# Block 0's loads of v placed ahead of the first pieces of w_in in the SyncE queue

## The chip, the cores and the metric

The kernel runs on one core of a Trainium2 chip. The metric is device time in microseconds (us) of one execution. A trace of one execution is taken with the hardware profiler; its span is about 1.75 us shorter than the time that is reported for the same execution. Such a profile of one execution is called a look below. PE is TensorE (matmul), PEld its weight loads, ACT ScalarE, DVE VectorE, POOL GpSimd, SP SyncE and SPq its queue of DMA issues.

## The reference

Attention inside chunks of 64 tokens, then a two-layer network with a gated activation on all 4608 tokens:

```python
# q, k, v: (8, 8, 576, 64); chunks of 64 tokens, no attention across chunks
scores = scale * np.matmul(q_c, k_c.transpose(0, 1, 2, 4, 3))
attn = np.exp(scores - np.max(scores, axis=-1, keepdims=True))
attn = attn / (np.sum(attn, axis=-1, keepdims=True) + 1e-09)
x = np.matmul(attn, v_c)         # reordered to (4608, 512)
...
h = x @ w_in                     # w_in: (512, 2048)
g = h * (1.0 / (1.0 + np.exp(-beta * h)))
out = g @ w_out                  # w_out: (2048, 512)
```

## The kernel before

The kernel is a list of events, each with a time on a fictive clock. Sorted by that time they give the program of every engine; waits on semaphores are derived from reads and writes. Tokens are worked in nine blocks of 512. Block 0 has to begin before its data are there, so its loads stand in the queue of SyncE in the order of need. v of block 0 is loaded in eight pieces of 128 KB: four for the heads of the first half (u=0), four for the second (u=1). w_in is loaded in column groups s of 512 columns; group 0 comes in four row pieces c of 256 KB, group 1 to 3 in two pieces of 512 KB each. The first piece of group 1 is called **e1a** below.

```python
for u in range(2):
    for m in range(4):
        at(-97.9, load_v_u, 0, m, u)            # eight pieces of v ...
    for c in ((0,), (1, 2, 3))[u]:
        at(-97.9, load_w_in, 0, c, 1)           # ... w_in piece 0 between the halves
for e0 in range(1, 4):
    for cp in range(2):
        at(-97.7, load_w_in, e0, 2 * cp, 2)     # groups 1 to 3; e1a is the first
...
for m in range(4):                              # POOL: casts to bf16
    at(8.6 + 0.1 * m - 100, cast_v_u, 0, m, 0, "pool")
    at(10.4 + 0.1 * m - 100, cast_v_u, 0, m, 1, "pool")
at(10 - 100, cast_w_in, 0, 0, ("pool",))
...
for t in range(4):                              # PE: first layer, group 0
    at(11.5 + 0.1 * t - 100, mm1, 0, t, (0,))   # after the attention of u=1 (11.21, 11.46)
    at(12.1 + 0.1 * t - 100, mm1, 0, t, (1,))
    at(14 + 0.5 * t - 100, mm1, 0, t, (2, 3))
```

PE works in program order: attention of u=1 (needs v, second half), then the four matmuls of w_in piece 0 and of piece 1 with the transposes of x between them, then pieces 2 and 3, then group 1.

The softmax here doesn't subtract the row's maximum and nothing guards it: scores larger than these inputs give would overflow.

## Time and profile before

| | before |
|---|---|
| time, median of 3 runs | 290.87 us (290.63 to 291.61) |
| profiled execution | 292.47 us, span 290.7 us |
| PE busy | 280.4 us, 96% of the span |
| last v piece of block 0 landed | 17.63 us |
| e1a landed | 22.04 us |

Busy time is time with an instruction on the engine; a busy PE can still be pipelined less than perfectly. The page also shows that the DMA engines carry more than the kernel's loads. It lists the DMA queues with their packets, bytes and share of the 16 engines' time:

```profile
q1 hardware_dynamic: 127264, 47.33, 74.5%
q10 hardware_dynamic: 5600, 9.84, 11.0%
q8 instruction: 17, 0.28, 0.5%
q14 instruction: 7, 0.06, 0.1%
```

q1 has SyncE's loads, q10 ACT's transfers, and the third line is 17 fetches of program code of 16 KB each. The first came at 15.06 us. The seven fetches of the last line have 8 KB each.

### The profile page before, as it was taken

How to read it: one execution, taken by the hardware profiler on the slowest of the kernel's cores; microseconds unless marked ns; L12 is line 12 of the kernel's file. 1: busy time of each engine (PE TensorE's matmuls, PEld its weight loads, DVE VectorE, ACT ScalarE, POOL GpSimd, SP SyncE). 2: the span in 40 equal slices, each digit the busy share in tenths (PEclk: the TensorE clock that was granted, in tenths of full speed). 3: DMA queues.
4: the chain of work that ended last, by engine and by line, in shares of the span. 5: the costliest groups of instructions: out<-in, count | busy, mean ns of one | idle time of the engine just before them, and what ended most of it. 6: DMA issues, size and time to landing. Idle time of an engine off the chain costs nothing.

```text
span 290.7 us, 5459 instructions
## 1 busy us (share of the span) xinstructions
PE 280.4 (96%) x2210; PEld 136.2 (47%) x2210; DVE 146.3 (50%) x289; ACT 159.0 (55%) x225; POOL 80.9 (28%) x126
## 2 busy tenths in 40 slices
PE   7669999999999999999999999999999999999995
PEld 3434445545544554445444544454445444544444
DVE  0736616585428452745285617561856086608601
ACT  2436606688247824782488347743874377528510
POOL 1548845734121442050114102410233020000000
PEclk9999999999999999999999999999999999999999
DMA  6999999999599999995999599949999891340033
GB/s 229 242 290 399 407 359 247 298 164 267 144 235 201 271 219 224 210 235 125 193 242 238 92 221 204 276 116 180 235 184 182 189 204 23 74 127 18 2 69 77
DMA packets 132888, 57.51 MB, mean 198 GB/s; under 512 B 116864, under 2 KB 123264, under 8 KB 132864
## 3 DMA queue, kind: packets, MB, share of 16 engines
q1 hardware_dynamic: 127264, 47.33, 74.5%
q10 hardware_dynamic: 5600, 9.84, 11.0%
q8 instruction: 17, 0.28, 0.5%
q14 instruction: 7, 0.06, 0.1%
HBM read 36.71 MB, written 9.44 MB: 159 GB/s over the span
## 4 chain that ended last, share of the span: by engine, by line
PE 90%; SPq 4%; DMA 3%; POOL 0%; issue 0%; ACT 0%; DVE 0%
PE F L492 42%; PE F L472 38%; PE A L472 4%; DMA wstage<-in_moe_w_in_dram 3%; PE A L408 2%; PE A L382 2%; SPq L354 2%; SPq L323 1%; PE F L517 1%; SPq L246 1%; PE A L340 1%; POOL w_in_bf L260 0%; ACT kT L258 0%; PE A L421 0%; PE F L451 0%
## 5 line engine op out<-in xcount | busy, mean ns | idle before, releaser
L492 PE MATMUL F<-w_out_bf,g 128*128 128x512 bf16 x560 | 129.2, 379 | 0.0
L485 DVE SCALAR_TENSOR_TENSOR g<-tt,F 128x512 bf16<-128x512 bf16 x132 | 89.9, 687 | 75.9 <-ACT tt L482 75.7
L472 PE MATMUL F<-xT,w_in_bf 128*128 128x512 bf16 x528 | 116.9, 379 | 0.2
L482 ACT ACTIVATE tt<-F,beta_half 128x512 bf16<-128x512 f32 x132 | 89.7, 687 | 26.9 <-PE F L472 26.8
L472 PEld LDWEIGHTS F<-xT,w_in_bf 128*128 128x128 bf16 x528 | 51.1, 98 | 61.9 <-issue 0.6
L492 PEld LDWEIGHTS F<-w_out_bf,g 128*128 128x128 bf16 x560 | 51.8, 98 | 56.4
L500 ACT ACTIVATE ostage<-F 128x512 f32<-128x512 f32 x33 | 19.6, 597 | 67.1 <-PE F L492 67.0
L260 POOL CAST vaug<-vstage 128x512 bf16<-128x512 f32 (+1 forms) x44 | 23.5, 537 | 80.1 <-DMA vstage<-in_v_dram 77.2
L403 ACT ACTIVATE wstage<-A 64x1024 bf16<-64x1024 f32 x28 | 28.5, 1018 | 5.2 <-PE A L382 4.7
L260 POOL CAST qcast<-qstage 128x1024 bf16<-128x1024 f32 (+1 forms) x18 | 17.0, 945 | 44.6 <-DMA qstage<-in_q_dram 43.5
L433 DVE TENSOR_TENSOR x_sb<-A,rden 128x256 bf16<-128x256 f32 (+1 forms) x62 | 27.9, 450 | 2.1
L431 DVE RECIPROCAL rden<-A 128x4 f32<-128x4 f32 (+1 forms) x62 | 11.2, 180 | 29.8 <-PE A L408 26.1
L260 POOL CAST kcast<-kstage 128x512 bf16<-128x512 f32 (+1 forms) x29 | 18.1, 628 | 25.2 <-DMA kstage<-in_k_dram 24.9
L408 PEld LDWEIGHTS A<-vaug,wstage 128*128 128x128 bf16 x224 | 10.8, 98 | 6.7 <-ACT wstage L403 1.7
L408 PE MATMUL A<-vaug,wstage 128*128 128x65 bf16 x224 | 11.7, 193 | 0.0
L472 PE MATMUL A<-xT,w_in_bf 128*128 128x512 bf16 x48 | 11.0, 379 | 0.2 <-POOL w_in_bf L260 0.2
L260 POOL CAST w_in_bf<-wstage 128x512 bf16<-128x512 f32 x16 | 9.5, 613 | 3.4 <-DMA wstage<-in_moe_w_in_dram 3.2
L482 ACT ACTIVATE tt<-A,beta_half 128x512 bf16<-128x512 f32 x12 | 8.0, 690 | 2.1 <-PE A L472 2.1
L485 DVE SCALAR_TENSOR_TENSOR g<-tt,A 128x512 bf16<-128x512 bf16 x12 | 7.8, 684 | 2.0 <-ACT tt L482 2.0
L260 POOL CAST w_out_bf<-wstage 128x1024 bf16<-128x1024 f32 x8 | 8.3, 1040 | 1.8 <-DMA wstage<-in_moe_w_out_dram 1.7
L382 PEld LDWEIGHTS A<-qT,kT 64*64 64x64 bf16 x576 | 6.2, 107 | 4.2 <-issue 3.0
L382 PE MATMUL A<-qT,kT 64*64 64x64 bf16 x576 | 7.5, 196 | 0.3 <-ACT kT L258 0.3
(52 smaller groups left out, 73.0 us busy)
## 6 DMA issues: line engine op xcount, KB each, us to landing
out_dram<-ostage ACTq DMA_DIRECT2D x32, 256.0 KB, 3.6
kstage<-in_k_dram SPq DMA_DIRECT2D x30, 256.0 KB, 6.5
qstage<-in_q_dram SPq DMA_DIRECT2D x12, 512.0 KB, 5.4
vstage<-in_v_dram SPq DMA_DIRECT2D x24, 256.0 KB, 4.9
wstage<-in_moe_w_out_dram SPq DMA_DIRECT2D x8, 512.0 KB, 12.6
vstage<-in_v_dram SPq DMA_DIRECT2D x24, 128.0 KB, 4.6
wstage<-in_moe_w_in_dram SPq DMA_DIRECT2D x6, 512.0 KB, 9.2
qstage<-in_q_dram SPq DMA_DIRECT2D x8, 256.0 KB, 9.0
```

Source lines behind the costliest of these rows:

```text
L260: P.op(eng, lambda e: e.tensor_copy(dst, src), reads=r, writes=wr)
L354: P.dma("sp", lambda e: e.dma_start(stages["v"][:, blk, 512 * m + 256 * u:512 * m + 256 * u + 256].rearrange("p (h d) -> p h d", d=64), v[ ...
L382: return e.matmul(A[64 * c2:64 * c2 + 64, bank, col:col + 64], turned["k"][r, hp, t], qq)
L403: P.op("act", lambda e: e.activation(dst, src, AF.Exp, scale=0.125), reads=[K("A", 2 * u + i, v=("s", blk)) for i in range(2)], writes=[K( ...
L408: P.op("pe", lambda e, h=h: e.matmul(A[:, bank, 128 * (h % 4):128 * (h % 4) + 65], EB[:, 16 * u + 8 * (h % 2) + 4 * (h // 2 % 2) + m, :], ...
L431: P.op("dve", lambda e: e.reciprocal(rd, o[:, :, :, 64]), reads=r, writes=[K("rden", m, u, v=blk) for m in ms])
L433: P.op("dve", lambda e: e.tensor_tensor(x_sb[:, ms[0]:ms[0] + n, 256 * u:256 * u + 256].rearrange("p b (h d) -> p b h d", h=4), o[:, :, :, ...
L472: P.op("pe", lambda e, c=c: e.matmul(ps[:, bank, :], w_in_bf[:, c, 256 * e0 + i:256 * e0 + 256:2], xT[:, c, :], start=(c == 0), stop=(c == ...
L482: P.op("act", lambda e: e.activation(tt[:, T % NTT, :], ps[:, bank, :], AF.Tanh, scale=beta_half[:, e0, i:i + 1]), reads=[K(*pkey(ps, bank ...
L485: P.op("dve", lambda e: e.scalar_tensor_tensor(g2[:, t, :], tt[:, T % NTT, :], 1.0, ps[:, bank, :], ALU.add, ALU.mult), reads=[K(*pkey(ps, ...
L492: P.op("pe", lambda e, t=t: e.matmul(F[:, s, :], g2[:, t, 128 * s:128 * s + 128], w_out_bf[:, t, :], start=(t == 0), stop=(t == NT - 1)), ...
L500: f = (lambda e: e.activation(dst, src, AF.Copy, scale=0.5)) if eng == "act" else \
```

## The change

The intent is to let the second half of v, which has attention, normalising and transposing behind it, go ahead of w_in piece 0. The cast of piece 0 moves behind the casts of v in POOL's program, and pieces 2 and 3 become one DMA.

```diff
         for u in range(2):
             for m in range(4):
                 at(-97.9, load_v_u, 0, m, u)
-            for c in ((0,), (1, 2, 3))[u]:
-                at(-97.9, load_w_in, 0, c, 1)
+        for c, n in ((0, 1), (1, 1), (2, 2)):
+            at(-97.8, load_w_in, 0, c, n)
...
-        at(10 - 100, cast_w_in, 0, 0, ("pool",))
+        at(11 - 100, cast_w_in, 0, 0, ("pool",))
```

The programs of PE, DVE and ACT are the same instruction for instruction.

## The prediction

> **What bounds the kernel now.** I read the page first: 290.7 us of span, PE (TensorE matmul) busy 280.4 us of it. Adding up the chain of work that ended last gives PE for 90% and the queue of SyncE (SPq) with its transfers for 7%. That 7% lies at the front, so I then read the chain in order of time from the start of the span to 26 us (columns: start us, us, what):
>
> ```profile
> 6.54 2.10 SPq L354
> 8.68 1.53 SPq L246
> ...
> 12.39 0.93 SPq L246
> ...
> 14.34 7.70 DMA wstage<-in_moe_w_in_dram
> 22.04 0.05 issue
> 22.09 1.18 POOL w_in_bf L260 x2
> ```
>
> L354 issues the pieces of v, L246 the pieces of w_in. Up to 22.04 us the end of the kernel hangs on SyncE's issues and one transfer: the first piece of w_in for column group 1 (call it e1a, 512 KB), issued at 14.34 and landed 7.70 us later. POOL casts its two halves and PE runs without gaps from 23.32 us: the chain has PE alone from there to 44.50 us. The change sits wholly ahead of that point, so its worth is **by how much 23.32 us moves**, if nothing behind takes it back.
>
> Next the timeline of PE and POOL between 14 and 24 us (start, duration, engine, line, operation; in brackets the idle time before it and who ended it):
>
> ```profile
> 14.12 0.40 POOL L260 CAST vaug<-vstage 128x256 bf16<-128x256 f32 x1
> ...
> 17.69 0.40 POOL L260 CAST vaug<-vstage 128x256 bf16<-128x256 f32 x1 [2.02 <-DMA vstage<-in_v_dram]
> 18.14 0.31 PE L421 MATMUL A<-vaug,E 64*64 64x65 bf16 x8 [2.07 <-POOL vaug L260]
> 18.22 1.29 POOL L260 CAST w_in_bf<-wstage 128x512 bf16<-128x512 f32 x2
> ...
> 20.59 0.61 POOL L260 CAST w_in_bf<-wstage 128x512 bf16<-128x512 f32 x1 [1.08 <-DMA wstage<-in_moe_w_in_dram]
> ...
> 22.78 0.38 PE L472 MATMUL A<-xT,w_in_bf 128*128 128x512 bf16 x1
> 23.32 3.41 PE L472 MATMUL A<-xT,w_in_bf 128*128 128x512 bf16 x15 [0.16 <-POOL w_in_bf L260]
> ```
>
> The 2.07 us in which PE waits for the last cast of v is the largest hole the change can touch. But it is not on the chain above: after it PE still has to wait for w_in, whose last pieces arrive later. Asking for the issues one by one gives each landing (issue + time to landing), in us: v first half 10.96, 11.51, 11.99, 12.44; w_in piece 0 13.48; v second half 14.06, 14.64, 15.19, **17.64**; w_in pieces 1, 2, 3 at 18.19, 18.87, 20.55; e1a 22.04; then one 512 KB piece each 1.35 us or so (23.41, 24.73, 26.12).
>
> Last, the table of stretches (length; busy us of PE, PEld, DVE, ACT, POOL; granted clock; DMA share; GB/s):
>
> ```profile
> 10.00:12.00 2.00, 1.73 (x50) 1.34 (x50) 1.06 (x5) 1.17 (x2) 0.97 (x3) 1.00 0.62 131
> 14.00:16.00 2.00, 1.57 (x34) 0.97 (x33) 1.10 (x4) 1.94 (x4) 1.31 (x4) 1.00 0.94 189
> 16.00:18.00 2.00, 0.07 (x6) 0.00 (x0) 0.89 (x2) 0.20 (x1) 0.31 (x1) 1.00 0.93 289
> 20.00:24.00 4.00, 3.69 (x20) 1.37 (x19) 2.02 (x4) 2.60 (x5) 2.35 (x5) 1.00 1.05 399
> ```
>
> From 20 us on the DMA engines are full at 399 GB/s; between 10 and 12 us they are busy 0.62 of the time although v and w_in had been issued. That is the slack a new order could win back.
>
> **What the Trainium skill says.** (1) "DMA: Bandwidth & Descriptors", section "Queues, rings and completion order": SP's transfers go onto one ring in each of the 16 engines, and each engine consumes its ring in order. The trace agrees: the landings above are in the order of issue, so moving a load ahead moves what it passes back. (2) Same page, "Why a DMA increments its semaphore by 16 and not by 1": only the full 16 means that all data landed. In the trace's record of partial completions, 15 of the 16 for the last piece of v are there by 15.68 us and the last comes at 17.63; a 16 KB instruction fetch starts at 15.06 and takes 1.53 us. I take it that the fetch sat on the engine of the straggler. (3) Same page, "Why small descriptors are slow (HBM only)": 256-byte pieces carry a fixed cost each. v moves in 256-byte packets; the packet records have about 18 ns for one, against about 88 ns for 2 KB of w_in. 512 packets over 16 engines at 18 ns are 0.58 us for 128 KB of v; 128 packets at 88 ns are 0.70 us for 256 KB of w_in. (4) "TensorE: Matmul & The Clock Gate", "The HAM clock gate": the clock drops after some 3.4 us idle. The 2.07 us hole left it at 1.00 in every stretch above, and I expect no longer hole.
>
> **The change, part by part.**
> *Nothing is removed from the work*: the same bytes and casts, and one DMA fewer, since w_in pieces 2 and 3 come as one 512 KB transfer. That saves one issue of 0.44 us and makes the cast of piece 2 wait for piece 3 as well.
> *v ahead of w_in piece 0.* From 12.44 us the slowest engine goes on with the second half of v instead of piece 0. With the old spacing of 0.55 (between the second-half landings) that gives 13.0, 13.5, 14.1, 14.65; I allow 15.0. This is ahead of the 15.06 us at which the fetch started, so the last piece of v loses its 17.64 landing: **2.6 to 3.0 us earlier**. Attention u=1 needs its exponentials as well (ACT ends them at 15.06), and its first 24 matmuls started at 15.50 behind the third cast. Now all 32 can go at about 15.2 to 15.9, and the 2.07 us hole closes.
> *w_in piece 0 behind v, with the cast behind it in POOL's order.* Free of the fetch it would land at 14.65 + 0.7 = 15.35, but the fetch now falls on this transfer: +1.5 us or somewhat more, 17.0 to 17.5. Cast 0.61: 17.6 to 18.1. PE's order puts the four matmuls of piece 0 ahead of the second-half transposes of x, so PE waits here instead: it starts at about 17.9, where the old kernel started at 18.39.
> *Pieces 1 and 2+3.* Piece 1 at +0.7 = 17.7 to 18.2. Pieces 2+3 at +1.35, 19.1, if all flows; the old piece 3 took 1.68 us behind piece 2 where 0.7 would do, so up to 20.1 if that second delay returns. Two casts at 0.61 behind it: c=3 ready at 20.3 to 21.3 (old: 21.20).
> *e1a.* The bytes ahead of it are the same, so only recovered idle time helps. +1.35 behind pieces 2+3: 20.5 to 21.5 against 22.04.
> *PE.* After c=3 is cast, seven matmuls at 0.216 us (3.45 us for 16 in the chain) end group 0: 1.5 us, so 21.8 to 22.8; e1a's two casts (1.18) are done at 21.7 to 22.7, just in time. The old kernel had one of the 16 matmuls of group 1 done when it began the gapless run at 23.32, so its equivalent start is 23.1. **Gain: 0.3 to 1.3 us, middle 0.8.**
> *What takes it back.* The next places where PE meets loads are in block 1: its last piece of v was cast on POOL at 50.89 to 51.29, and the attention that needs it ran at 52.18, so 0.9 us of slack; other waits of PE there were at most 0.25 us. These loads come from the same queue and also move a little ahead. I take off about a third: **0.5 us gained, 290.87 - 0.5 = 290.4**.
>
> **The rivals.**
> *A: the wait is only moved* (for: e1a at 22.04 is on the chain and its bytes ahead are unchanged; PE is in order and waits for piece 0 behind the same fetch). Then e1a stays at 22.0, pieces 2+3 at 20.5, c=3 is cast at 21.75, group 0 ends at 23.3: 0.2 us *lost*, about 291.1. Against: 0.62 share at 10 to 12 us and the long gaps of pieces 3 and e1a are not work.
> *B: the full gain of the hole*, 2.07 us, 288.8. It needs e1a two us earlier, landing at 20.0; against: the rate behind 20 us is already 399 GB/s, and the fetch of 1.53 us still stands in some transfer's way.
> *C: worse flow*: eight v pieces of 512 small packets in a row. The fourth issue of v already took 2.10 us where 0.51 is usual, and the one after it 1.53[...]. If the second half blocks SyncE for 1 to 2 us more and the other 15 engines run dry, e1a comes 0.5 to 1 us later: 291.5 to 292. Against: the queue then holds work for every engine, and w_in behind it needs only 128 packets for 256 KB.
>
> **Range and chances.** I give the middle account 0.5, A 0.3, B 0.07, C 0.13. The runs of before themselves spread from 290.63 to 291.61. This makes 290.4 the middle, 289.3 to 291.4 for 8 in 10. Two per cent are 5.8 us: more than all idle time of PE between 12 and 23 us, so faster by 2% has 0.01. Slower by 2% needs a stall of 5.8 us that nothing in the profile suggests: 0.01.
>
> **What would show it right or wrong.** Right: the cast of the last v piece starts by 15.3 us instead of 17.69; no PE hole of 2 us ahead of the second-half attention, but one of 1.3 to 2 us ahead of the first matmul of piece 0; e1a lands between 20.5 and 21.5; the gapless run starts 0.3 to 1.3 us earlier and that lead is still there, less a third, at 60 us. Wrong: v's last piece still late (the fetch, or a later start of it, still hits v); e1a at 22.0 (rival A) or later with longer SPq issues at L354 (rival C); or the lead is there at 24 us and gone by 57 us, where block 1's loads set the pace.

## The result, and the profile after

The changed kernel took 290.76 us (median of 6 runs, 290.21 to 291.37) against 290.97 us (6 runs, 290.47 to 291.64). The ratio is 0.999 with a 95% interval of 0.997 to 1.0011: no difference that this comparison can tell from noise. A ratio here is the mean time of one kernel's fast runs over that of the other's in the same rounds, so it is not quite the ratio of the medians that I quote. The profiled execution had a span of 289.6 us, 1.1 us less than that of before. So there are two findings to reconcile: a profile that gained 1.1 us and medians that gained 0.2.

The chain of work that ended last, after (start us, us, what):

```profile
8.33 1.51 SPq L354
...
11.54 0.51 SPq L246
...
12.56 6.65 DMA wstage<-in_moe_w_in_dram
...
19.26 1.18 POOL w_in_bf L260 x2
...
20.49 1.69 PE F L472 x7
22.18 3.45 PE A L472 x16
```

The DMA on the chain is now the merged pieces 2+3 of group 0, issued at 12.56 us, and no longer e1a. PE ends group 0 and goes straight into group 1 at 22.18 us. In the timeline of PE and POOL (start, duration, engine, line, operation; idle time before it and who ended it in brackets):

```profile
15.46 0.40 POOL L260 CAST vaug<-vstage 128x256 bf16<-128x256 f32 x1 [0.98 <-DMA vstage<-in_v_dram]
...
15.91 0.31 PE L421 MATMUL A<-vaug,E 64*64 64x65 bf16 x8 [0.25 <-POOL vaug L260]
...
16.80 1.04 PE L472 MATMUL F<-xT,w_in_bf 128*128 128x512 bf16 x4 [0.57 <-POOL w_in_bf L260]
...
19.26 1.17 POOL L260 CAST w_in_bf<-wstage 128x512 bf16<-128x512 f32 x2 [1.84 <-DMA wstage<-in_moe_w_in_dram]
19.93 0.39 PE L472 MATMUL F<-xT,w_in_bf 128*128 128x512 bf16 x1 [0.79 <-POOL w_in_bf L260]
```

The wait of 2.07 us ahead of the last attention has become one of 0.25 us, and new waits of 0.57 and 0.79 us stand ahead of w_in piece 0 and piece 2. The stretches that answer to those of before (length; busy us of PE, PEld, DVE, ACT, POOL; granted clock; DMA share; GB/s):

```profile
10.00:12.00 2.00, 1.74 (x50) 1.11 (x46) 1.50 (x5) 1.57 (x3) 1.22 (x3) 1.00 1.03 196
16.00:18.00 2.00, 1.43 (x17) 0.84 (x18) 1.32 (x3) 0.00 (x0) 1.23 (x2) 1.00 1.00 281
20.00:24.00 4.00, 3.83 (x18) 1.65 (x19) 2.36 (x4) 2.42 (x4) 3.35 (x7) 1.00 1.05 397
```

The DMA share between 10 and 12 us is 1.03 where before showed 0.62. e1a landed at 20.66 us, 1.38 us earlier. From group 1 on the two traces run in parallel: the second layer of block 0 begins at 32.37 us (before 33.47), the first layer of block 2 at 81.67 (82.77), the last matmul at 286.11 (287.21). The lead of 1.10 us is neither lost nor widened anywhere behind 32 us.

### The profile page after: what moved, and what is told of

It reads as the page before. It is cut to its first block, busy times and chain, and to the rows that moved or that the text cites. A ratio compares the mean times of both kernels' runs of the same rounds, so it can differ in the third digit from the quotient of the medians.

```text
span 289.6 us, 5460 instructions
## 1 busy us (share of the span) xinstructions
PE 280.8 (97%) x2210; PEld 136.5 (47%) x2210; DVE 146.2 (50%) x289; ACT 159.0 (55%) x225; POOL 81.0 (28%) x126
## 4 chain that ended last, share of the span: by engine, by line
PE 91%; SPq 4%; DMA 2%; POOL 0%; ACT 0%; issue 0%; DVE 0%
PE F L492 42%; PE F L472 39%; PE A L472 4%; PE A L408 2%; DMA wstage<-in_moe_w_in_dram 2%; SPq L354 2%; PE A L382 2%; SPq L323 1%; PE F L517 1%; PE A L340 1%; POOL w_in_bf L260 0%; ACT kT L258 0%; PE A L421 0%; SPq L246 0%; PE F L451 0%
## 5 line engine op out<-in xcount | busy, mean ns | idle before, releaser
L403 ACT ACTIVATE wstage<-A 64x1024 bf16<-64x1024 f32 x28 | 28.5, 1018 | 5.2 <-PE A L382 4.7
L260 POOL CAST kcast<-kstage 128x512 bf16<-128x512 f32 (+1 forms) x29 | 18.1, 628 | 23.2 <-DMA kstage<-in_k_dram 23.0
```

The costliest lines, as they stand in the source:

```text
L260: P.op(eng, lambda e: e.tensor_copy(dst, src), reads=r, writes=wr)
L403: P.op("act", lambda e: e.activation(dst, src, AF.Exp, scale=0.125), reads=[K("A", 2 * u + i, v=("s", blk)) for i in range(2)], writes=[K( ...
```

## The experiments

Theory 1: the profile of before was an ordinary execution, the new order is about 1 us faster, and the spread of the runs hid it. Theory 2: that profile was an unlucky execution of the old order and the order is worth little. Rival causes inside the change are the merged DMA and the place of an instruction fetch. Twelve kernels ran in three jobs, each on a chip of its own; all gave correct results. Each job has 11 runs of the kernel before and 6 of each of its four kernels. Runs in the slow state (one each of e7 and e10) are left out of means and ratios but not of medians, and e10's single look fell in such a run.

### e1_null: the kernel before, unchanged

> The kernel before, unchanged, timed against itself: ratio 1.000, and its width is what the other runs of this job have to beat. Its profile is a second look at the old order. Theory 1 (the profile of before was an ordinary execution): the last piece of v again lands near 17.6 us, e1a (first w_in piece of column group 1) near 22.0, PE's gapless run of group 1 again stands for a start of 23.1 us, span near 290.7. Theory 2 (that profile was an unlucky execution, which is why the profiles differ by 1.1 us and the medians by 0.2): the last piece of v lands by 16.5, e1a by 21.2, span near 289.3.

No edit. Ratio 0.9988 (0.9953 to 1.0024), median 291.04 us. The look at the old order was quite another one: the last v piece landed at 15.40, e1a at 20.34, span 289.1. Its timeline and its stretch from 10 to 12 us:

```profile
15.45 0.31 PE L421 MATMUL A<-vaug,E 64*64 64x65 bf16 x8 [0.19 <-POOL vaug L260]
...
21.63 0.61 PE L472 MATMUL A<-xT,w_in_bf 128*128 128x512 bf16 x2 [0.17 <-POOL w_in_bf L260]
```

```profile
10.00:12.00 2.00, 1.68 (x46) 1.00 (x44) 1.50 (x5) 1.85 (x3) 1.42 (x4) 1.00 1.05 209
```

No 2 us hole ahead of the attention, and no idle DMA engines between 10 and 12 us. Group 1 went into its gapless run at 21.63 us, earlier than in the first look at the changed kernel. **So the hole, the late v piece and the 0.62 share, on which the prediction rested, were marks of one execution and not of the old order as such.** As to the profile of before, theory 2 is right; of the 45 timed runs of the old order in all comparisons four were longer than its 292.47 us.

### e2_after_again: the changed kernel again

> The changed kernel again. Theory 1: it is really about 1 us faster and the first comparison was blurred by the spread: ratio 0.9965 or so. Theory 2: ratio 0.999 to 1.000. In both its profile should have the last v piece by 16.2 us, e1a at 20.3 to 21.0 and group 1 from about 22.2.

No edit. Ratio 0.9974 (0.9942 to 1.0007), median 290.76, range 290.40 to 291.16. The last v piece landed at 13.87, e1a at 19.87, the second matmul of group 1 began at 21.53. Between the two theories by its ratio; the interval holds both 1.000 and 0.9965.

### e3_order_only: no merged DMA

```diff
-        for c, n in ((0, 1), (1, 1), (2, 2)):
-            at(-97.8, load_w_in, 0, c, n)
+        for c in range(4):
+            at(-97.8, load_w_in, 0, c, 1)
```
(against the changed kernel)

> The change without the merged transfer: all of v ahead, then four single pieces of w_in group 0, cast of piece 0 behind v. If the order is what matters and the merge is neutral: within 0.1 per cent of the changed kernel; piece 2 cast about 0.6 us before piece 3 instead of both behind one landing, so PE ends group 0 up to 0.5 us sooner than in the changed kernel, if e1a allows it. If the merge mattered (one DMA fewer): e1a 0.3 us or more later than in the changed kernel.

Ratio 0.9974 (0.9938 to 1.0011), median 291.01, range 290.13 to 291.57. As with the merge: the order alone gives the ratio of the changed kernel. Group 1 came 0.2 us sooner than in e2 (second matmul at 21.35 against 21.53), but the first layer of block 1 began 0.9 us later (51.64 against 50.75), because PE waited for v of block 1.

### e4_merge_only: the old order with the merged DMA

```diff
-            for c in ((0,), (1, 2, 3))[u]:
-                at(-97.9, load_w_in, 0, c, 1)
+            for c, n in (((0, 1),), ((1, 1), (2, 2)))[u]:
+                at(-97.9, load_w_in, 0, c, n)
```
(against the kernel before)

> The kernel before with pieces 2 and 3 of w_in as one transfer, nothing else. If the order carries the gain of the profile: as before, ratio 0.999 to 1.002, the last v piece still late whenever the instruction fetch falls on it, PE ending group 0 up to 0.5 us later. If the merge carries it: e1a below 21.2 us and a ratio like the changed kernel's.

Ratio 1.0004 (0.9966 to 1.0041), median 291.75, and four of six runs above 291.6 us. The merge is not what helps the time. In its look the front was as good as in e2 (e1a at 20.10, second matmul of group 1 at 21.39), yet the span was 290.1. The timeline at the second half of v of block 1 shows where the lead went:

```profile
50.83 0.75 POOL L260 CAST vaug<-vstage 128x256 bf16<-128x256 f32 x2 [3.08 <-DMA vstage<-in_v_dram]
51.29 0.66 PE L421 MATMUL A<-vaug,E 64*64 64x65 bf16 x16 [0.97 <-POOL vaug L260]
```

PE waited 0.97 us for the last v pieces of block 1. That is the take-back that the prediction had allowed for; it exists, but only in some executions.

### e5_v_last: all of group 0 ahead of the second half of v

```diff
-            for c in ((0,), (1, 2, 3))[u]:
+            for c in ((0, 1, 2, 3), ())[u]:
```
(against the kernel before)

> The opposite order: all four w_in pieces of column group 0 ahead of the second half of v. Theory 1 (the place of v counts, because the last v piece has a chain of attention, normalising and transposing behind it, while e1a, first w_in piece of group 1, has the same bytes ahead of it in any order): e1a at 20.1 to 21.0 as in the other looks, the last v piece at 17.9 to 18.7, PE idle 3 us or more ahead of the second-half attention, group 1 begun only at 22.5 to 23.2 instead of 21.3 to 22.2: ratio 1.003 to 1.005. Theory 2 (only e1a counts): group 1 begun at 21.3 to 22.2, ratio 0.998 to 1.001.

Slower by more than either theory had it: ratio 1.0103 (1.0073 to 1.0132), median 295.11. e1a landed at 19.63 us, the earliest of all looks, and the last v piece at 18.28; still the second matmul of group 1 began only at 24.92. So it is not e1a alone that counts: v's place does too, through its chain of attention, normalising and transposing. The expected start was 22.5 to 23.2. Two stretches of this look show the rest:

```profile
15.13:18.54 3.41, 0.86 (x24) 0.61 (x24) 0.22 (x2) 0.20 (x1) 1.39 (x4) 1.00 1.03 261
18.54:21.95 3.41, 3.24 (x24) 1.61 (x19) 1.58 (x3) 0.45 (x1) 3.41 (x7) 0.50 0.95 294
```

PE was busy for 0.86 of 3.41 us, waiting twice for v (1.82 and 1.09 us), and for the next 3.41 us the granted clock was 0.50. Work that fills 3.41 us at half the clock would take 1.7 us less at the full one, which is about what the expectation was short of (1.7 to 2.4 us). By this estimate a good part of this look's loss comes from the clock, and not from v's chain directly. All six runs had a mean clock of 0.987 to 0.994, where 0.998 to 1.000 is usual.

### e6_fetch_moved_old and e7_fetch_moved_new: the instruction fetch moved

```diff
+        def spin4(n, ps, bank):
+            for i in range(4 * n):
+                P.op("pe", lambda e, i=i: e.matmul(ps[:, bank, 128 * (i % 4):128 * (i % 4) + 128],
+                                                   identity[:, :], identity[:, :]),
+                     reads=[K("identity")], writes=[K(*pkey(ps, bank), v="spin")])
...
-        at(-99.2, spin, 14, A, 3)
+        at(-99.2, spin4, 14, A, 3)
```
(e6 against the kernel before, e7 against the changed kernel)

e6:

> The kernel before with its 14 first warm-up matmuls of 512 columns cut into 56 of 128 columns (84 instructions more on PE in the same time), so the first instruction fetch comes earlier: at 11 to 13 us instead of 14.1 to 16.0. If the fetch that falls on or near the last v piece makes the long executions of the old order: last v piece by 15.6, mean time near 290.8 and no run above 291.6 (23 runs of the old order have 8 above 291.5, 12 of the changed kernel none). If it does not matter what the fetch falls on, as long as it is ahead of e1a: mean near 291.3 and long runs as before.

e7:

> The same cut of the warm-up matmuls in the changed kernel. Both accounts: the fetch at 11 to 13 us falls on a v piece that has slack; mean 290.6 to 290.9, as the changed kernel. If the fetch on w_in pieces had held back group 1: e1a 0.5 us or more earlier than the 19.9 to 20.7 of the two looks so far and a mean near 290.3.

The fetch moved as meant, to 11.87 and 11.70 us. Everything else was a miss. e6 got slower, ratio 1.0058 (1.0029 to 1.0086), all six runs above 292.5 us; e7 was at 0.9994 (0.9961 to 1.0028), median 292.58, with a slow run left out of the ratio. Moving the first fetch also moved the second, from between 25.4 and 28.5 us in the other looks of fast runs to 21.4 and 21.6 us, on top of w_in pieces that have little slack. In e7:

```profile
24.83 0.39 PE L478 MATMUL A<-xT,w_in_bf 128*128 128x512 bf16 x1 [0.28 <-POOL w_in_bf L260]
25.38 0.82 PE L478 MATMUL A<-xT,w_in_bf 128*128 128x512 bf16 x3 [0.17 <-POOL w_in_bf L260]
```

PE now waits inside group 1, which none of the three looks at the changed kernel shows. In both kernels one of the 16 completions of a v piece came more than 1 us behind the other 15 (in e6 at 14.65, the fifteenth at 13.46), as in the first look at before. Here the delay goes with a fetch in time; the trace does not name the engine of a packet, so that it is the same engine is argued and not shown. The edit was no clean test either: four of six runs of e6 had a mean clock of 0.994 or less, so the new warm-up may also have disturbed the clock. I cannot say from these two what the fetch costs the old order.

### e8_stores_later: block 1 relieved

```diff
-                    at(28 if early else 32 * blk + 16 + n if blk else 32.6, store, blk, s)
+                    at(32.55 if early else 32 * blk + 16 + n if blk else 32.6, store, blk, s)
```
(against the changed kernel)

> The changed kernel with the first two output stores (512 KB, issued at about 43 to 45 us on ACT) moved behind the other two of block 0, at about 51 us. If the lead won at the front is taken back in part of the executions by the second half of v of block 1 (two looks show PE waiting for it): those pieces land about 1 us earlier (last by 49.2), no PE wait for them, median 0.1 to 0.4 us below the changed kernel. If not: the same median within 0.15 us, or slower by up to 0.5 if the stores now collide with the loads of block 2.

Ratio 0.996 (0.9938 to 0.9981), median 290.85, range 290.41 to 291.05. The last cast of block 1's v began at 48.08 us where the first look at the changed kernel had 50.10, and PE did not wait for it. That is no proof of the edit: e2 and e9, the changed kernel with its stores in their old place, have this cast at 47.43 and 47.99, and PE did not wait for it in any look at the changed kernel. Besides, the kernel before ran at 291.92 us on this chip, so the ratio mixes the order with the stores; the next job separates them.

### e9 to e12: order and stores side by side

e9:

> The changed kernel a third time, beside the three that follow. If the new order cuts the long executions of the old one (so far: old order up to 294.07, changed kernel at most 291.37 in 12 runs): mean 290.6 to 290.9 with none above 291.6, against a mean near 291.3 to 291.9 for the kernel before: ratio 0.996 to 0.998. If the narrow spread of the first 12 runs was luck: spread as wide as before's and ratio 0.999 to 1.001.

e10:

> The kernel before (old order) with the first two output stores moved to about 51 us, nothing else. If the long executions of the old order come from the front, up to the start of group 1: as before, ratio 0.999 to 1.001, several runs above 291.6. If they come from block 1's second half of v behind the stores: mean near 290.8, ratio 0.996 to 0.998, spread as narrow as the changed kernel with later stores.

e11:

> The changed kernel with later stores again, now on the chip of the changed kernel itself. If block 1's v takes back a part of the lead in some executions: 0.1 to 0.3 us below the changed kernel of this job, ratio 0.995 to 0.997 to the kernel before. If the later stores change nothing: equal to the changed kernel within 0.1 us.

e12:

> All of v ahead, four single w_in pieces instead of the merged one, and later stores. The single piece 2 is cast before piece 3 lands, so PE ends group 0 up to 0.5 us sooner; the look without later stores began group 1 at about 21.1 us but lost 0.9 us to block 1's v. If later stores keep that lead: span 288.5 to 289.0 and 0.1 to 0.3 us below the changed kernel with later stores. If group 1 is set by e1a anyway: equal to it within 0.15 us.

e9 is the changed kernel, e11 is e8 again, e10 and e12 are the edit of e8 on the kernel before and on e3.

| run | order of v | stores | ratio (95%) | median us | range of fast runs |
|---|---|---|---|---|---|
| e9_after_third | ahead | as they were | 0.9968 (0.9937 to 0.9999) | 290.81 | 290.26 to 291.58 |
| e10_old_stores_later | as before | later | 1.0 (0.9947 to 1.0052) | 292.62 | 289.81 to 293.90 |
| e11_new_stores_later | ahead | later | 0.9973 (0.9943 to 1.0002) | 291.19 | 290.20 to 291.82 |
| e12_single_stores_later | ahead, no merge | later | 0.9969 (0.993 to 1.0008) | 290.30 | 289.99 to 292.62 |

The median of e10 includes its slow run. Later stores don't narrow the old order's spread, which speaks against block 1 as the only source of its long runs, and they don't make the new order faster: e11 is not below e9, against its expectation. e12 has four runs from 289.99 to 290.34 and two at 292.6; its mean of 290.97 is no better than e9's 290.91. No version of this job beats the changed kernel in the mean.

e10's look fell in a slow run, so I read it for what can happen and not for a difference in time. e1a landed at 22.86 us there:

```profile
18.00:20.00 2.00, 1.87 (x12) 0.82 (x11) 0.42 (x1) 0.63 (x2) 1.10 (x2) 1.00 0.53 155
```

```profile
23.59 0.39 PE L472 MATMUL A<-xT,w_in_bf 128*128 128x512 bf16 x1 [2.42 <-POOL w_in_bf L260]
```

The DMA engines were busy about half the time while w_in was queued behind, and PE waited 2.42 us. It looks like the starvation in the first look at before, at another place. The wait also cost clock (columns as above):

```profile
21.71:25.12 3.41, 1.37 (x6) 0.60 (x7) 1.40 (x3) 0.62 (x2) 2.03 (x4) 1.00 1.05 392
25.12:28.53 3.41, 3.41 (x10) 1.21 (x8) 0.52 (x1) 1.08 (x2) 2.86 (x6) 0.50 1.05 399
```

The low mean clock of this run (0.994) comes from this one stretch, which lies behind the late load and so can't have caused it. A halved clock is not what makes the other long runs: of the old order's 19 runs above 291.6 us whose clock is on record, one alone (294.07 us, 0.993) has a mean clock below 0.998.

### All looks and all runs together

Landings in us; "group 1" is the start of its second matmul; "lag" is how far, for the first v piece, the last of the 16 completions came behind the fifteenth. Only kernels with the usual warm-up and v not last:

| look | order | lag | last v | e1a | group 1 | span |
|---|---|---|---|---|---|---|
| before | old | 0.96 | 17.63 | 22.04 | 23.32 | 290.7 |
| e1_null | old | 0.47 | 15.40 | 20.34 | 21.63 | 289.1 |
| e4_merge_only | old | 0.27 | 14.88 | 20.10 | 21.39 | 290.1 |
| e10 (slow run) | old | 0.55 | 15.89 | 22.86 | 24.14 | 293.6 |
| after | new | 0.42 | 15.40 | 20.66 | 22.23 | 289.6 |
| e2_after_again | new | 0.21 | 13.87 | 19.87 | 21.53 | 288.9 |
| e8_stores_later | new | 0.05 | 14.25 | 20.14 | 21.81 | 289.2 |
| e9_after_third | new | 0.05 | 14.07 | 19.89 | 21.55 | 289.0 |
| e11_new_stores_later | new | 0.34 | 14.29 | 20.48 | 22.13 | 289.6 |
| e3_order_only | new, no merge | 0.31 | 14.29 | 20.07 | 21.35 | 289.8 |
| e12 | new, no merge | 0.72 | 14.62 | 22.15 | 23.44 | 290.9 |

(Some matmul records are missing in the traces of e9 to e12; the first two of group 1 are there.) With the new order and the merge e1a stays within 19.87 and 20.66; in the others it can be two us later. With so few looks this is a hint.

The times say more. The unchanged old order ran 45 times in these comparisons (6, 11, 11, 11, and 6 in e1): mean 291.56 us, 21 runs above 291.6, up to 294.07. The changed kernel ran 18 times (6 each in the first comparison, e2 and e9): mean 290.82, **none above 291.58**. Kept to the three comparisons that hold both kernels it is 34 runs with mean 291.47 and 14 above 291.6, against the same 18: if the kernels did not differ, a split with all 14 on one side would come up about once in 1300 draws. Drawn within each comparison, so that the chips don't enter, it is about once in 1400. The cut at 291.6 was chosen after the first two comparisons; e9 is the one test that was forecast with it, and it came out as told (7 of 11 runs above, against none of 6). The gain of the mean is 0.65 us, or 0.2%. The short executions are hardly shorter (290.47 against 290.21): **the new order cuts long executions rather than speeding up the good ones.** The order seems to carry this and not the merge: e3 has no run above 291.6, e4 has four of six. But it is fewer long executions and not none: with later stores the new order has one of six above 291.6 (e11) and, without the merge, two of six (e12).

## Why the prediction was right or wrong

The time was inside the range (290.76 in 289.3 to 291.4), and no change of 2% was forecast or found. By its steps:

- **The last v piece at 14.65 to 15.0**: it landed at 15.40 in the first look, 13.87 to 14.29 in the later ones. Right in kind, but in the first look its cast began at 15.46 and not by 15.3, behind a wait of 0.98 us on POOL. "2.6 to 3.0 us earlier" was 2.2 against the look at before and nothing against e1 (15.40).
- **The fetch falls on piece 0, which lands at 17.0 to 17.5, with a PE hole of 1.3 to 2 us ahead of its first matmul**: wrong. The fetch came at 16.01 us and not at 15.06; piece 0 landed at 16.08 and the hole was 0.57 us. The delay fell on pieces 2+3 (19.21, inside the 19.1 to 20.1 told) with PE waiting 0.79 us there. In the later looks at the changed kernel the last of the 16 completions of pieces 2+3 came 1.89 us (e2) and 1.62 us (e9) behind the fifteenth, and PE waited 1.62 and 1.44 us.
- **e1a at 20.5 to 21.5**: 20.66. **Group 0 ended at 21.8 to 22.8**: 22.18. **Gapless run 0.3 to 1.3 us earlier**: 1.10 us by the second layer of block 0. All right for these two traces.
- **"Gain: 0.3 to 1.3 us" against the kernel before** failed as a step: its base was not typical. The other look at the old order has group 1 at 21.63 us, ahead of the changed kernel's first look. The 2.07 us hole and the DMA share of 0.62, called "the slack a new order could win back", are absent from it. The share was misread besides: not all of v and w_in "had been issued". The second half of v was issued only from 10.26 us, behind issues of 2.10 and 1.53 us (in e1 from 9.57, behind 1.24 and 1.54, with a share of 1.05); what made these issues long is not shown. What the runs show in its place is a mean gain of 0.65 us by fewer long executions; that the predicted 0.5 us lies near it is partly luck.
- **"I take off about a third"** for block 1: in the first look nothing was taken back (1.10 us at 32 us and at 286 us). In e4 a wait of 0.97 us was. It is an event of some executions and not a share of the gain.
- **Rival A** (the wait only moves) describes the good executions of the two kernels well in kind, though not in its numbers (e1a at 22.0): e2 and e1 differ by 0.1 us at group 1. **Rival B** was excluded rightly. **Rival C**: the fifth issue of v did take 1.51 us where 0.51 is usual, but e1a was then issued earlier and not later; SyncE was through with all issues of w_in by 17.98 us instead of 19.13.
- **The clock**: at 1.00 through the front in the changed kernel, as told. The worry was sound, but the length of a single hole was the wrong test: the waits of e5 that halved the clock (1.82 and 1.09 us, close together) are each shorter than the 2.07 us hole of before, which did not.

What stays open is why the old order has more long executions. The place of e1a against the first fetch does not sort the looks: it was issued ahead of the fetch in all of the table but e10 (at 14.34 us in before, 14.05 in e1, 13.04 in the changed kernel, 13.59 in e12), and moving the fetch (e6, e7) gave no clean answer. The lag of the first v piece does: the three looks with e1a at 22 us or later are the three with the largest lag (0.96, 0.72 and 0.55 us), and it stands there at about 10.5 us, well ahead of any fetch in the span. That is a mark found afterwards in eleven looks, and no cause; e12 has it with the new order. The trace would have to name the engine of each packet.

## What to carry to other kernels

A hole in one profile is a property of one execution until a second profile of the same kernel shows it: profile the unchanged kernel twice before working out what a change wins back, and compare the profiled run's time with the timed ones. When a reorder leaves the bytes ahead of the bound transfer as they were, expect little in the good executions, and look at the spread: what has the longest chain behind it should land with slack, so that a stray delay falls on something that can wait. That is the reading that the runs leave, and not one that they prove. Do not buy that slack with a longer PE hole, since in two looks (e5, e10) a poorly filled 3.4 us cost half the clock for the next 3.4 us.

## What the Trainium skill lacked or had wrong

- That program code is fetched in blocks of 16 KB by a DMA queue of its own is told in "Runtime: NRT & Kernel Launch", section "Instruction fetch mechanics", which calls the cost mostly hidden. No page tells what a kernel's own loads can lose at that time. Here 17 blocks were fetched in a run (18 in e6 and e7), the first at 14 to 16 us in kernels with the usual warm-up and taking 0.92 to 1.66 us. In seven of these twelve looks a load in flight at that time had its last of 16 completions 1.46 to 1.95 us behind the fifteenth, in the other five at most 0.87. That the fetch causes it is not shown.
- "TensorE: Matmul & The Clock Gate", section "HAM oscillation", gives the rule of no PE idle gaps above about 3.4 us. It is not enough, and the page's next section, "A second HAM failure mode: psum-queue depth-cycling", itself tells of short pauses that did it: in e5 the longest single gap was 1.82 us, in e10 2.42, and the clock was halved all the same. The length of the drop (3.41 us) and its depth (0.50) agree with the page. The page does not say how much work keeps the clock. With every trace but e7's, which has no clock records, cut into stretches of 3.41 us from its first clock record, PE was busy for 1.42 us or less in each stretch ahead of a half-clock one (0.86 in e5, 1.37 in e10) and for 1.67 us or more ahead of each full-clock one (1.82 in before, with most of its hole).
- No page tells when an issue on SyncE blocks. Here issues that usually take 0.43 to 0.6 us took longer behind the first loads of v, of 512 packets each: 0.54 to 2.10 us for the fourth issue of v and 1.50 to 1.86 us for the one behind it, in all looks.
